# Whole loads of wo and w1, a bf16 turn of the result, and 3/8 of w2's last block in small loads on four DMA engines

## The chip, the cores and the metric

One core of a Trainium2 chip. The metric is the device time of one execution in microseconds (us). A run also has a span, which the profile takes over the program's own instructions; the time is longer than the span by 1.25 to 1.4 us in most runs, and that surplus becomes a subject below. Before: 420.07 us, the median of 3 runs (420.02 to 420.12).

## The reference

A decode step for two sequences of one token: a modulated layernorm, attention of 32 query heads over 4 cached key and value heads of 32768 positions, then an MLP with gelu. Cut to what matters:

```python
mod = (_silu(c) @ w_mod).reshape(c.shape[0], 6, 1, -1)      # sa, ca, ga, sb, cb, gb
h = _layernorm(x) * (1 + ca) + sa
x = x + ga * attention(h, k_cache, v_cache, wq, wo)          # wo: 4096 x 1024
h = _layernorm(x) * (1 + cb) + sb
x = x + gb * (gelu(_layernorm(h) @ w1 + b1) @ w2 + b2)       # w1: 1024 x 3584, w2: 3584 x 1024
```

All is bf16. A "turn" below is a transpose made on TensorE. 178 MB are read, 134 MB of them the caches; the last 22 MB are wo (8), w1 (7) and w2 (7).

## The kernel before

All big operands pass through one ring of 160 KB per partition, in the order wmod, wq, eight rounds of K, K, V, wo, w1, w2. An item is loaded as soon as the readers of what stood in its place are done. What the change touches:

```python
W2_ITEMS = ((0, 8, 96), (8, 16, 112), (16, 24, 128), (24, 27, 144), (27, 28, 150))   # blocks, place in KB
# ...
for m, off in enumerate((128, 0)):
    add(("wo", m), [16, DM], A_wo[m * 2048:(m + 1) * 2048, :].rearrange("(p j) n -> p j n", j=16), off * KB)
w1_v = B_w1.rearrange("(p k) n -> p k n", k=KT8)
for m, off in enumerate((32, 64)):
    add(("w1", m), [4, F], w1_v[:, 4 * m:4 * m + 4, :], off * KB)
w2_v = B_w2.rearrange("(p j) n -> p j n", j=FT)
for m, (j0, j1, off) in enumerate(W2_ITEMS):
    add(("w2", m), [j1 - j0, DM], w2_v[:, j0:j1, :], off * KB)
# ... attention, wo, layernorm, w1, gelu -> gT ...
for g in range(16):                       # blocks 0-15 as rows: gT is the stationary operand
    for hf in range(2):
        # ... pe: matmul(psS[0][32*t : 32*t+32, :], lhsT=gT[:, g, :], rhs=w[:, j, hf*512:(hf+1)*512])
load_row("dve", psS[0], "psS0", 3)        # copy out of PSUM
to_columns(psO, "psO", 3, True, False)    # four f32 matmuls turn the rows into columns
for g in range(16, FT):                   # blocks 16-27 as columns: w2 is the stationary operand
    for k in range(KT8):
        # ... pe: matmul(psO[:, 2*k:2*k+2], lhsT=w[:, j, k*128:(k+1)*128], rhs=gT[:, g, 0:2])
# dve: mT = psO * gb ; res_bf = mT + x1b
pe(lambda e: e.matmul(psM[0:16, 0:128], lhsT=res_bf.rearrange("p b k -> p (b k)"), rhs=ident[:, :], start=True, stop=True),
   reads=["res_bf", "ident"], writes=["psM"])
dve(lambda e: e.tensor_copy(res16[:, :], psM[0:16, 0:128]), reads=["psM"], writes=["res16", "c16"])
```

Below, "item one" to "item five" are the five loads of w2.

## Time and profile before

| | before |
|---|---|
| time, median of 3 | 420.07 us |
| span of the profile | 418.7 us |
| DMA | busy in all 40 slices, 426 GB/s over the span |
| last load of w2 lands | 415.76 us |
| result stored | 418.7 us |

The profile's page and its views are quoted in the prediction, with what each line says. Two things are needed besides. Each load leaves landing marks in the trace, taken here as one for each DMA engine that it uses (16 for item four; the four-row load of b2 has 4 and an early one), in the order of time and without the engine's number; a load counts as landed with the last. And the chain of waits gives, for each piece, start, length and what was done or waited for; "DMA w" is the wait for a load of w1 or w2.

### The profile page before, as it was taken

Reading aid. Unit: us, or ns where it says so; the run is one execution under the profiler, and the core shown is the slowest. Engines: PE = TensorE matmul, PEld = TensorE weight load, DVE = VectorE, ACT = ScalarE, POOL = GpSimd, SP = SyncE. Lnnn points to the kernel's source line nnn. Section 1 sums busy time; section 2 is a strip of 40 time slices with the busy share of each in tenths; the row PEclk is TensorE's granted clock in tenths of the full one; section 3 lists DMA queues with packets and bytes.
Section 4 is the critical chain, followed back from the end, with each engine's and each line's share of the span. In section 5 each row is a group of like instructions: output and inputs, shape, how many; then the busy total and the mean of one; then the engine's idle time right before and its main releaser. Section 6 shows DMA issues by size and latency. Waiting matters only on the chain.

```text
span 418.7 us, 11609 instructions
## 1 busy us (share of the span) xinstructions
PE 291.0 (70%) x5183; PEld 231.3 (55%) x5183; DVE 209.6 (50%) x423; ACT 149.4 (36%) x179; POOL 6.8 (2%) x29
## 2 busy tenths in 40 slices
PE   1407449766996895699369957976995699564536
PEld 1104219762993794299149926962894399221214
DVE  1201105546677676467726664766477567620411
ACT  2000015533565364256405632643365166400100
POOL 3000000000000000000000000000000000000000
PEclk9999557986896997799589958986697889576585
DMA  9989999999999999999999999999999999899995
GB/s 373 450 380 449 448 404 493 398 406 446 441 432 429 423 451 429 419 454 457 391 435 476 407 416 448 438 438 426 438 438 426 416 460 457 377 448 428 424 427 249
DMA packets 5581, 178.42 MB, mean 426 GB/s; under 512 B 698, under 2 KB 706, under 8 KB 964
## 3 DMA queue, kind: packets, MB, share of 16 engines
q1 hardware_dynamic: 5572, 178.28, 98.8%
q8 instruction: 8, 0.13, 0.1%
q14 instruction: 1, 0.01, 0.0%
HBM read 178.28 MB, written 0.00 MB: 426 GB/s over the span
## 4 chain that ended last, share of the span: by engine, by line
DMA 71%; PE 24%; DVE 2%; issue 1%; ACT 1%; SPq 1%
DMA V<-in_A_v_cache_dram 39%; DMA wo<-in_A_wo_dram 10%; DMA K<-in_A_k_cache_dram 10%; PE psZ L584 10%; DMA w<-in_B_w_dram 9%; PE psKT L536 8%; DMA wmod<-in_w_mod_dram 4%; PE psS L548 1%; PE psZ L548 1%; PE psS L655 1%; PE psZ L729 1%; PE psZ L469 1%; ACT KT_sb L540 0%; PE psS L469 0%; DVE m1c L553 0%
## 5 line engine op out<-in xcount | busy, mean ns | idle before, releaser
L536 PE MATMUL psKT<-ident,K 128*128 128x128 bf16 x2048 | 163.1, 229 | 11.5 <-DMA K<-in_A_k_cache_dram 11.5
L540 ACT ACTIVATE KT_sb<-psKT 128x1024 bf16<-128x1024 bf16 x96 | 98.2, 1025 | 124.4 <-PE psKT L536 124.4
L542 DVE COPY KT_sb<-psKT 128x1024 bf16<-128x1024 bf16 x160 | 106.7, 688 | 61.6 <-PE psKT L536 61.2
L536 PEld LDWEIGHTS psKT<-ident,K 128*128 128x128 bf16 x2048 | 126.7, 102 | 13.0 <-DMA K<-in_A_k_cache_dram 12.7
L584 PE MATMUL psZ<-V,E_sb 128*32 128x512 bf16 x512 | 46.4, 541 | 23.2 <-DMA V<-in_A_v_cache_dram 20.0
L548 PE MATMUL psS<-qcur,KT_sb 128*128 128x8 bf16 x1024 | 44.7, 167 | 2.2 <-issue 2.2
L584 PEld LDWEIGHTS psZ<-V,E_sb 128*32 128x32 bf16 x512 | 18.7, 130 | 47.7 <-issue 38.8
L548 PE MATMUL psZ<-qcur,KT_sb 128*128 128x8 bf16 x1024 | 43.0, 167 | 2.2 <-issue 1.5
L548 PEld LDWEIGHTS psS<-qcur,KT_sb 128*128 128x128 bf16 x1024 | 40.0, 97 | 2.3 <-issue 2.3
L548 PEld LDWEIGHTS psZ<-qcur,KT_sb 128*128 128x128 bf16 x1024 | 37.9, 96 | 3.4 <-issue 1.6
L572 ACT ACTIVATE E_sb<-S_sb 128x512 bf16<-128x512 f32 x32 | 19.5, 630 | 29.6 <-DVE S_sb L570 29.6
L570 DVE TENSOR_TENSOR S_sb<-S_sb,gmb 128x512 f32<-128x512 f32 x32 | 20.0, 685 | 0.3
L576 DVE TENSOR_REDUCE rs<-E_sb 128x8 f32<-128x512 bf16 x32 | 19.7, 675 | 0.0
L469 PE MATMUL psS<-wmod,inT 128*32 128x512 bf16 x32 | 5.1, 624 | 16.2 <-DMA wmod<-in_w_mod_dram 16.2
L553 DVE TENSOR_REDUCE m1c<-psZ 128x8 f32<-128x512 f32 x16 | 11.1, 693 | 10.2 <-ACT S_sb L552 10.1
L595 DVE RECIPROCAL rinv<-psM 128x1 f32<-128x1 f32 x8 | 1.3, 168 | 27.7 <-PE psM L593 27.7
L605 PE MATMUL psM<-msum,hmat 128*128 128x128 f32 x16 | 4.2, 347 | 13.3 <-DVE msum L600 13.3
L559 PE MATMUL psM<-identf,m 128*8 128x128 f32 x16 | 4.3, 369 | 13.1 <-DVE m L556 13.1
L553 DVE TENSOR_REDUCE m1c<-psS 128x8 f32<-128x512 f32 x16 | 11.1, 693 | 3.2 <-ACT S_sb L552 3.1
L552 ACT ACTIVATE S_sb<-psZ 128x512 f32<-128x512 f32 x16 | 9.5, 595 | 7.5 <-PE psZ L548 7.5
L477 DVE COPY S_sb<-psS 128x512 f32<-128x512 f32 x1 | 0.7, 690 | 22.9 <-PE psS L469 22.9
L469 PEld LDWEIGHTS psS<-wmod,inT 128*32 128x32 bf16 x32 | 1.1, 132 | 19.3 <-DMA wmod<-in_w_mod_dram 18.0
(123 smaller groups left out, 167.5 us busy)
## 6 DMA issues: line engine op xcount, KB each, us to landing
K<-in_A_k_cache_dram SPq DMA_DIRECT2D x16, 4096.0 KB, 27.1
wq<-in_A_wq_dram SPq DMA_DIRECT2D x2, 4096.0 KB, 44.8
wo<-in_A_wo_dram SPq DMA_DIRECT2D x2, 4096.0 KB, 39.0
w<-in_B_w_dram SPq DMA_DIRECT2D x2, 3584.0 KB, 32.5
wmod<-in_w_mod_dram SPq DMA_DIRECT2D x1, 6144.0 KB, 29.8
w<-in_B_w_dram SPq DMA_DIRECT2D x3, 2048.0 KB, 37.8
wmod<-in_w_mod_dram SPq DMA_DIRECT2D x1, 4608.0 KB, 15.8
wmod<-in_w_mod_dram SPq DMA_DIRECT2D x1, 1536.0 KB, 6.0
```

Source lines behind the costliest of these rows:

```text
L469: pe(lambda e, w=it.view, k=k, kk=kk, ch=ch, n=n, q=q: e.matmul(bank[n][32 * q:32 * q + 32, :], lhsT=inT[:, k, :], rhs=w[:, kk, ch * 512:( ...
L536: pe(lambda e, kq=kq, jj=jj, w=kt, t=t: e.transpose(psKT[kq][:, jj * 128:(jj + 1) * 128], w[:, t, :], ident[:, :]), reads=[it.reg, "ident" ...
L540: act(lambda e, src=src: e.activation(KT_sb[g8][:, :, :], src, ACT.Copy), reads=[f"psKT{kq}"], writes=[f"KT_sb{g8}"], sem=f"ev{cc}_{g8}")
L542: dve(lambda e, src=src: e.tensor_copy(KT_sb[g8][:, :, :], src), reads=[f"psKT{kq}"], writes=[f"KT_sb{g8}"], sem=f"ev{cc}_{g8}")
L548: pe(lambda e, t=t, jj=jj: e.matmul(ps[:, t * HPG:(t + 1) * HPG], lhsT=KT_sb[g8][:, jj, :], rhs=qcur[:, :], start=True, stop=True), reads= ...
L552: act(lambda e: e.activation(Sc, ps.rearrange("p (t h) -> p h t", h=HPG), ACT.Copy), reads=[preg], writes=[f"S_sb_{cc}"], sem=f"sc{cc}")
L553: dve(lambda e: e.tensor_reduce(m1c[:, :, cc], ps.rearrange("p (t h) -> p h t", h=HPG), AX.X, ALU.max), reads=[preg], writes=[f"m1c{cc}"])
L559: pe(lambda e: e.matmul(psM[0:HPG, 0:128], lhsT=m1[:, :], rhs=identf[:, :], start=True, stop=True), reads=["m1", "identf"], writes=["psM"])
L570: dve(lambda e: e.tensor_tensor(Sc, Sc, gmb[:, :].unsqueeze(2).to_broadcast([128, HPG, TPC]), ALU.subtract), reads=[f"S_sb_{cc}", "gmb"], ...
L572: act(lambda e: e.activation(Ec, Sc.rearrange("p h (u t) -> p u h t", t=4), ACT.Exp, scale=SCALE), reads=[f"S_sb_{cc}"], writes=[f"E_sb_{c ...
L576: dve(lambda e: e.tensor_reduce(rs4[:, :, cc], Ec.rearrange("p u h t -> p h u t"), AX.XY, ALU.add), reads=[f"E_sb_{cc}"], writes=[f"rs4_{c ...
L584: pe(lambda e, t4=t4, tg=tg, q=q: e.matmul(psO[32 * q:32 * q + 32, :], lhsT=E_sb[:, tg // 4, :, :].rearrange("p h t -> p (h t)"), rhs=vt[: ...
```

## The change

The intent: half of the 16 DMA engines end 1.3 us before the other half, so part of the last bytes is moved to four engines, by small loads into partitions 0-15 and 32-47; fewer, longer loads for wo and w1; a cheaper last copy. Two row blocks of w2 become column blocks. The core of the diff, with the tables of the attention output (which now hold four groups instead of two) cut:

```diff
-W2_ITEMS = ((0, 8, 96), (8, 16, 112), (16, 24, 128), (24, 27, 144), (27, 28, 150))
+W2_ITEMS = ((0, 8, 64), (8, 16, 80), (16, 24, 0), (24, 27, 16), (27, 28, 22))
+W2_ROWS = 14
+W2_CUT = 640
 ...
-    for m, off in enumerate((128, 0)):
-        add(("wo", m), [16, DM], A_wo[m * 2048:(m + 1) * 2048, :]..., off * KB)
-    for m, off in enumerate((32, 64)):
-        add(("w1", m), [4, F], w1_v[:, 4 * m:4 * m + 4, :], off * KB)
+    add(("wo", 0), [32, DM], A_wo.rearrange("(p j) n -> p j n", j=32), 0)
+    add(("w1", 0), [8, F], B_w1.rearrange("(p k) n -> p k n", k=KT8), 104 * KB)
     for m, (j0, j1, off) in enumerate(W2_ITEMS):
-        add(("w2", m), [j1 - j0, DM], w2_v[:, j0:j1, :], off * KB)
+        n1 = W2_CUT if j1 == FT else DM
+        add(("w2", m), [j1 - j0, n1], w2_v[:, j0:j1, 0:n1], off * KB)
 ...                                          # after the matmuls of wo:
+    for q in range(4):
+        for h in range(2):
+            src = w2_v[32 * q + 16 * h:32 * q + 16 * h + 16, FT - 1, W2_CUT:DM].rearrange("(b a) n -> a b n", a=4)
+            T.dma("sp", ... e.dma_start(w2x[32 * h:32 * h + 16, q, :], src), ...)
 ...                                          # 14 row blocks; before the ninth: gx = the rows of gT that belong to w2x
+            for q in range(4):
+                pe(... e.matmul(psM[0:48, 56 + 2 * q:58 + 2 * q], lhsT=selp[:, q, :], rhs=gT[:, FT - 1, 0:2], ...))
 ...                                          # blocks 14 and 15 as columns, then
+    for q in range(4):
+        for k in range(W2_CUT // 128, KT8):
+            pe(... e.matmul(psO[:, 2 * k:2 * k + 2], lhsT=w2x[:, q, ...], rhs=gx[:, q, :], start=False, stop=False))
 ...
-    pe(... e.matmul(psM[0:16, 0:128], lhsT=res_bf..., rhs=ident[:, :], start=True, stop=True) ...)
-    dve(lambda e: e.tensor_copy(res16[:, :], psM[0:16, 0:128]), ...)
+    pe(... e.transpose(psKT[0][0:16, 0:128], res_bf..., ident[:, :]) ...)
+    dve(lambda e: e.tensor_copy(res16[:, :], psKT[0][0:16, 0:128]), ...)
```

More of the change, by code (lines that the diff above doesn't have):

```diff
@@ L258, in bass_adaLN_cond__gqa_block_cached__mixer_channel_mlp__decode_kernel @@
     onesf = sb("onesf", [128, 128])
-    hmat = sb("hmat", [128, 2, HPG, 8])
+    hmat = sb("hmat", [128, G, HPG, 4])
     hsel = sb("hsel", [128, HPG])
     mk4 = sb("mk4", [128, 4])
-    m8 = sb("m8", [128, 8])
+    m8 = sb("m8", [128, 4])
     mblk = sb("mblk", [128, KT8])
@@ L265, in bass_adaLN_cond__gqa_block_cached__mixer_channel_mlp__decode_kernel @@
     c16 = sb("c16", [16, 128], BF16)
-    rsum16 = sb("rsum16", [128, 2, HPG, 8])
+    rsum16 = sb("rsum16", [128, G, HPG, 4])
     msum = sb("msum", [128, 128])
@@ L289, in bass_adaLN_cond__gqa_block_cached__mixer_channel_mlp__decode_kernel @@
     qcur = sb("qcur", [128, HPG], BF16)
-    at = sb("at", [128, 16], BF16)
-    atT = [sb(f"atT{i}", [128, 16, 32], BF16) for i in range(G // 2)]
+    at = sb("at", [128, 32], BF16)
+    atT = sb("atT", [128, 32, 32], BF16)
     half = sb("half", [128, 2, 2])
@@ L301, in bass_adaLN_cond__gqa_block_cached__mixer_channel_mlp__decode_kernel @@
     res16 = c16
+    w2x = sb("w2x", [48, 4, DM - W2_CUT], BF16)
+    gx = sb("gx", [48, 4, 2], BF16)
+    selp = sb("selp", [128, 4, 48], BF16)
     m1c = sb("m1c", [128, HPG, NCH])
@@ L367, in bass_adaLN_cond__gqa_block_cached__mixer_channel_mlp__decode_kernel @@
         add_v(i)
-    for m, off in enumerate((128, 0)):
-        add(("wo", m), [16, DM], A_wo[m * 2048:(m + 1) * 2048, :].rearrange("(p j) n -> p j n", j=16), off * KB)
-    w1_v = B_w1.rearrange("(p k) n -> p k n", k=KT8)
-    for m, off in enumerate((32, 64)):
-        add(("w1", m), [4, F], w1_v[:, 4 * m:4 * m + 4, :], off * KB)
+    add(("wo", 0), [32, DM], A_wo.rearrange("(p j) n -> p j n", j=32), 0)
+    add(("w1", 0), [8, F], B_w1.rearrange("(p k) n -> p k n", k=KT8), 104 * KB)
     w2_v = B_w2.rearrange("(p j) n -> p j n", j=FT)
     for m, (j0, j1, off) in enumerate(W2_ITEMS):
-        add(("w2", m), [j1 - j0, DM], w2_v[:, j0:j1, :], off * KB)
+        n1 = W2_CUT if j1 == FT else DM
+        add(("w2", m), [j1 - j0, n1], w2_v[:, j0:j1, 0:n1], off * KB)
     w2_of = {j: (m, j - j0) for m, (j0, j1, off) in enumerate(W2_ITEMS) for j in range(j0, j1)}
@@ L411, in bass_adaLN_cond__gqa_block_cached__mixer_channel_mlp__decode_kernel @@
     T.inst("pool", lambda e: e.memset(onesf[:, :], 1.0), writes=["onesf"])
-    for t, nm in [(inT, "inT"), (gT, "gT")] + [(atT[g], f"atT{g}") for g in range(G // 2)]:
+    T.inst("pool", lambda e: e.memset(selp[:, :, :], 0.0), writes=["selp"])
+    for h in range(2):
+        T.inst("pool", lambda e, h=h: e.tensor_copy(selp[:, :, 32 * h:32 * h + 16].rearrange("p q (a b) -> p q a b", a=4),
+                                                    ident.rearrange("p (q h b a) -> p h q a b", q=4, h=2, a=4)[:, h]),
+               reads=["ident"], writes=["selp"])
+    T.inst("pool", lambda e: e.memset(w2x[:, :, :], 0.0), writes=["w2x"])
+    for t, nm in ((inT, "inT"), (gT, "gT"), (atT, "atT")):
         T.inst("pool", lambda e, t=t: e.memset(t[:, :, :], 0.0), writes=[nm])
@@ L451, in bass_adaLN_cond__gqa_block_cached__mixer_channel_mlp__decode_kernel @@
     dve(lambda e: e.tensor_reduce(hsel[:, :], identf.rearrange("p (c h t) -> p h c t", c=4, h=HPG), AX.XY, ALU.add), reads=["identf"], writes=["hsel"])
-    dve(lambda e: e.tensor_copy(hmat[:, :, :, :], hsel[:, :].unsqueeze(1).unsqueeze(3).to_broadcast([128, 2, HPG, 8])), reads=["hsel"], writes=["hmat"])
-    dve(lambda e: e.tensor_reduce(m8[:, :], identf.rearrange("p (h e) -> p e h", e=8), AX.X, ALU.add), reads=["identf"], writes=["m8"])
+    dve(lambda e: e.tensor_copy(hmat[:, :, :, :], hsel[:, :].unsqueeze(1).unsqueeze(3).to_broadcast([128, G, HPG, 4])), reads=["hsel"], writes=["hmat"])
+    dve(lambda e: e.tensor_reduce(m8[:, :], identf.rearrange("p (h e) -> p e h", e=4), AX.X, ALU.add), reads=["identf"], writes=["m8"])
     dve(lambda e: e.tensor_reduce(mblk[:, :], identf.rearrange("p (k u) -> p k u", u=16), AX.X, ALU.add), reads=["identf"], writes=["mblk"])
@@ L527, in next_q @@
         b, g = i % 2, i // 2
-        T.inst("pool", lambda e: e.tensor_copy(qcur[:, :], qT[:, b, g * HPG:(g + 1) * HPG]), reads=["qT"] + [f"atT{g}" for g in range(G // 2)], writes=["qcur"], sem="qc")
+        T.inst("pool", lambda e: e.tensor_copy(qcur[:, :], qT[:, b, g * HPG:(g + 1) * HPG]), reads=["qT", "atT"], writes=["qcur"], sem="qc")
     def tr(i, cc, g8):
@@ L591, in row_sums @@
         dve(lambda e: e.tensor_reduce(rowsum[:, :], rs4[:, :, :], AX.X, ALU.add), reads=[f"rs4_{cc}" for cc in range(NCH)], writes=["rowsum"])
-        dve(lambda e: e.tensor_copy(rsum16[:, :, :, :], rowsum[:, :].unsqueeze(1).unsqueeze(3).to_broadcast([128, 2, HPG, 8])), reads=["rowsum"], writes=["rsum16"], sem="rs")
+        dve(lambda e: e.tensor_copy(rsum16[:, :, :, :], rowsum[:, :].unsqueeze(1).unsqueeze(3).to_broadcast([128, G, HPG, 4])), reads=["rowsum"], writes=["rsum16"], sem="rs")
         pe(lambda e: e.matmul(psM[:, 144:145], lhsT=rsum16.rearrange("p g h e -> p (g h e)"), rhs=onesf[:, 0:1], start=True, stop=True),
@@ L606, in extract_2 @@
            reads=["hmat", "msum"], writes=["psM"])
-        dve(lambda e: e.scalar_tensor_tensor(out=pick[:, :, :], in0=psM[:, 256:384].rearrange("p (e j) -> p e j", j=16), scalar=rinv[:, 0:1],
-                                             in1=m8[:, :].unsqueeze(2).to_broadcast([128, 8, 16]), op0=ALU.mult, op1=ALU.mult),
+        dve(lambda e: e.scalar_tensor_tensor(out=pick.rearrange("p e j -> p (e j)").rearrange("p (e j) -> p e j", j=32), in0=psM[:, 256:384].rearrange("p (e j) -> p e j", j=32), scalar=rinv[:, 0:1],
+                                             in1=m8[:, :].unsqueeze(2).to_broadcast([128, 4, 32]), op0=ALU.mult, op1=ALU.mult),
             reads=["psM", "rinv", "m8"], writes=["pick"], sem="pk")
@@ L612, in red @@
             with nc.allow_low_precision("one nonzero term in each sum"):
-                return e.tensor_reduce(at[:, :], pick.rearrange("p e j -> p j e"), AX.X, ALU.add)
+                return e.tensor_reduce(at[:, :], pick.rearrange("p e j -> p (e j)").rearrange("p (e j) -> p j e", j=32), AX.X, ALU.add)
         dve(red, reads=["pick"], writes=["at"])
-        lo = 64 * (g % 2)
-        T.inst("pool", lambda e: e.tensor_copy(atT[g // 2][lo:lo + 64, :, b], at[lo:lo + 64, :]), reads=["at"], writes=[f"atT{g // 2}"], sem="ac")
+        lo = 32 * g
+        T.inst("pool", lambda e: e.tensor_copy(atT[lo:lo + 32, :, b], at[lo:lo + 32, :]), reads=["at"], writes=["atT"], sem="ac")
     rounds = {}
@@ L648, in bass_adaLN_cond__gqa_block_cached__mixer_channel_mlp__decode_kernel @@
     T.dma("sp", lambda e: e.dma_start(b1m[:, :], B_b1.rearrange("(q r) -> q r", r=448)), key="ld_b1", writes=["b1m"])
-    for m in range(2):
-        it = need("wo", m)
-        for j in range(16):
-            for hf in range(2):
-                q = 2 * (j % 2) + hf
-                pe(lambda e, w=it.view, m=m, j=j, hf=hf, q=q: e.matmul(psS[0][32 * q:32 * q + 32, :], lhsT=atT[m][:, j, :], rhs=w[:, j, hf * 512:(hf + 1) * 512],
-                                                                       start=(m == 0 and j < 2), stop=(m == 1 and j >= 14), skip_group_check=True),
-                   reads=[it.reg, f"atT{m}"], writes=["psS0"], mark=(j == 15 and hf == 1))
+    it = need("wo", 0)
+    for j in range(32):
+        for hf in range(2):
+            q = 2 * (j % 2) + hf
+            pe(lambda e, w=it.view, j=j, hf=hf, q=q: e.matmul(psS[0][32 * q:32 * q + 32, :], lhsT=atT[:, j, :], rhs=w[:, j, hf * 512:(hf + 1) * 512],
+                                                              start=(j < 2), stop=(j >= 30), skip_group_check=True),
+               reads=[it.reg, "atT"], writes=["psS0"], mark=(j == 31 and hf == 1))
+    for q in range(4):
+        for h in range(2):
+            src = w2_v[32 * q + 16 * h:32 * q + 16 * h + 16, FT - 1, W2_CUT:DM].rearrange("(b a) n -> a b n", a=4)
+            T.dma("sp", lambda e, q=q, h=h, src=src: e.dma_start(w2x[32 * h:32 * h + 16, q, :], src), key=f"ld_w2x{q}{h}", reads=["w2x"], writes=[f"w2x{q}{h}"])
     def load_row(e_name, b, b_reg, n, parts=128):
@@ L691, in bass_adaLN_cond__gqa_block_cached__mixer_channel_mlp__decode_kernel @@
     for k in range(KT8):
-        it = need("w1", k // 4)
+        it = need("w1", 0)
         for n in range(2):
@@ L695, in bass_adaLN_cond__gqa_block_cached__mixer_channel_mlp__decode_kernel @@
                 lo = 896 * q + 448 * n
-                pe(lambda e, w=it.view, k=k, n=n, q=q, lo=lo: e.matmul(zbank[n][32 * q:32 * q + 32, 0:448], lhsT=inT[:, k, :], rhs=w[:, k % 4, lo:lo + 448],
+                pe(lambda e, w=it.view, k=k, n=n, q=q, lo=lo: e.matmul(zbank[n][32 * q:32 * q + 32, 0:448], lhsT=inT[:, k, :], rhs=w[:, k, lo:lo + 448],
                                                                        start=False, stop=(k == KT8 - 1), skip_group_check=True),
@@ L713, in bass_adaLN_cond__gqa_block_cached__mixer_channel_mlp__decode_kernel, with w2_columns @@
     dve(lambda e: e.tensor_tensor(x1b[:, :, :], x1b[:, :, :], x1T[:, :, :], ALU.add), reads=["x1b", "x1T"], writes=["x1b"])
-    for g in range(16):
+    def w2_columns(g, start):
+        m, j = w2_of[g]
+        it = need("w2", m)
+        for k in range(KT8 if g < FT - 1 else W2_CUT // 128):
+            pe(lambda e, w=it.view, g=g, j=j, k=k: e.matmul(psO[:, 2 * k:2 * k + 2], lhsT=w[:, j, k * 128:(k + 1) * 128], rhs=gT[:, g, 0:2],
+                                                            start=(start and k == 0), stop=(g == FT - 1 or (g == FT - 2 and k >= W2_CUT // 128)), skip_group_check=True),
+               reads=[it.reg, "gT"], writes=["psO"], mark=((k == KT8 - 1 and g in (15, 23, 26)) or (g == FT - 1 and k == W2_CUT // 128 - 1)))
+    for g in range(W2_ROWS):
+        if g == 8:
+            for q in range(4):
+                pe(lambda e, q=q: e.matmul(psM[0:48, 56 + 2 * q:58 + 2 * q], lhsT=selp[:, q, :], rhs=gT[:, FT - 1, 0:2], start=True, stop=True),
+                   reads=["selp", "gT"], writes=["psM"], mark=(q == 3))
+            act(lambda e: e.activation(gx[:, :, :], psM[0:48, 56:64].rearrange("p (q b) -> p q b", b=2), ACT.Copy), reads=["psM"], writes=["gx"])
         m, j = w2_of[g]
@@ L720, in bass_adaLN_cond__gqa_block_cached__mixer_channel_mlp__decode_kernel @@
             pe(lambda e, w=it.view, g=g, j=j, hf=hf, t=t: e.matmul(psS[0][32 * t:32 * t + 32, :], lhsT=gT[:, g, :], rhs=w[:, j, hf * 512:(hf + 1) * 512],
-                                                                   start=(g < 2), stop=(g >= 14), skip_group_check=True),
-               reads=[it.reg, "gT"], writes=["psS0"], mark=(hf == 1 and g in (7, 15)))
+                                                                   start=(g < 2), stop=(g >= W2_ROWS - 2), skip_group_check=True),
+               reads=[it.reg, "gT"], writes=["psS0"], mark=(hf == 1 and g in (7, W2_ROWS - 1)))
@@ L723, in bass_adaLN_cond__gqa_block_cached__mixer_channel_mlp__decode_kernel @@
     load_row("dve", psS[0], "psS0", 3)
-    to_columns(psO, "psO", 3, True, False)
-    for g in range(16, FT):
-        m, j = w2_of[g]
-        it = need("w2", m)
-        for k in range(KT8):
-            pe(lambda e, w=it.view, g=g, j=j, k=k: e.matmul(psO[:, 2 * k:2 * k + 2], lhsT=w[:, j, k * 128:(k + 1) * 128], rhs=gT[:, g, 0:2],
-                                                            start=False, stop=(g == FT - 1), skip_group_check=True),
-               reads=[it.reg, "gT"], writes=["psO"], mark=(k == KT8 - 1 and g in (23, 26, 27)))
+    for g in range(W2_ROWS, 16):
+        w2_columns(g, g == W2_ROWS)
@@ new lines, in bass_adaLN_cond__gqa_block_cached__mixer_channel_mlp__decode_kernel @@
+    for q in range(4):
+        for k in range(W2_CUT // 128, KT8):
+            pe(lambda e, q=q, k=k: e.matmul(psO[:, 2 * k:2 * k + 2], lhsT=w2x[:, q, k * 128 - W2_CUT:(k + 1) * 128 - W2_CUT], rhs=gx[:, q, :],
+                                            start=False, stop=False, skip_group_check=True),
+               reads=[f"w2x{q}0", f"w2x{q}1", "w2x", "gx"], writes=["psO"], mark=False)
+    to_columns(psO, "psO", 3, False, False)
+    for g in range(16, FT):
+        w2_columns(g, False)
@@ L732, in bass_adaLN_cond__gqa_block_cached__mixer_channel_mlp__decode_kernel @@
     dve(lambda e: e.tensor_tensor(mT[:, :, :], psO[:, 0:16].rearrange("p (k b) -> p k b", b=2), mod(5), ALU.mult), reads=["psO", "modT"], writes=["mT"])
     dve(lambda e: e.tensor_tensor(res_bf.rearrange("p b k -> p k b"), mT[:, :, :], x1b[:, :, :], ALU.add), reads=["mT", "x1b"], writes=["res_bf"])
-    pe(lambda e: e.matmul(psM[0:16, 0:128], lhsT=res_bf.rearrange("p b k -> p (b k)"), rhs=ident[:, :], start=True, stop=True),
-       reads=["res_bf", "ident"], writes=["psM"])
-    dve(lambda e: e.tensor_copy(res16[:, :], psM[0:16, 0:128]), reads=["psM"], writes=["res16", "c16"])
+    pe(lambda e: e.transpose(psKT[0][0:16, 0:128], res_bf.rearrange("p b k -> p (b k)"), ident[:, :]), reads=["res_bf", "ident"], writes=["psKT0"])
@@ L738, in bass_adaLN_cond__gqa_block_cached__mixer_channel_mlp__decode_kernel @@
+    dve(lambda e: e.tensor_copy(res16[:, :], psKT[0][0:16, 0:128]), reads=["psKT0"], writes=["res16", "c16"])
     s_out = nc.alloc_semaphore("s_out")
```

## The prediction

A is 415.47 - 415.12 = +0.35, less 0.08 and 0.06, so +0.2 on 420.07; B is -0.06 - 0.08 - 0.06 = -0.2; 419.9 was forecast. That C's extra matmuls would raise the clock is the author's estimate. In before, each of the 18 rises from half to full clock follows a step of 3.41 us with the PE busy for 80 to 100% of it; the step from 408.98 was busy for 2.62 of 3.42 us, 77%, and half clock followed.

> **What bounds the kernel now.** I read the page first: the slices and the DMA queues.
>
> ```profile
> DMA  9989999999999999999999999999999999899995
> GB/s 373 450 380 449 448 404 493 398 406 446 441 432 429 423 451 429 419 454 457 391 435 476 407 416 448 438 438 426 438 438 426 416 460 457 377 448 428 424 427 249
> ...
> q1 hardware_dynamic: 5572, 178.28, 98.8%
> q8 instruction: 8, 0.13, 0.1%
> ...
> HBM read 178.28 MB, written 0.00 MB: 426 GB/s over the span
> ```
>
> The 16 DMA engines are busy from the first slice to the last but one, so the span is the bytes at about 430 GB/s, plus what lies before the first byte and after the last. The change removes no bytes. It can only win or lose in the last microseconds, so next the chain of waits over the last 6 us (start, length, what):
>
> ```profile
> 375.40 37.83 DMA w<-in_B_w_dram
> 413.23 0.05 issue
> 413.27 1.87 PE psZ L729 x64
> 415.14 0.03 issue
> 415.17 1.03 PE psZ L729 x32
> 416.20 0.02 issue
> 416.22 0.19 DVE mT L732
> ...
> 416.43 0.24 DVE res_bf L733
> ...
> 416.72 0.29 PE psM L734
> ...
> 417.03 0.28 DVE c L736
> ```
>
> w2's third item (blocks 16 to 23) lands at 413.23 and 64 matmuls on columns follow, then the rest. Then a closing chain of four short operations, about 1.1 us, and the store (median 1.4 us to landing). The view of the tile w (count, min/median/max ns, first and last start) and the timeline near the end say how that work runs:
>
> ```profile
> L729 PE MATMUL psZ<-gT,w x96: 165/165/188, 413.3 to 416.0; 128*128 128x2 bf16 x96
> ...
> L720 PE MATMUL psS<-w,gT x32: 377/498/634, 403.7 to 409.7; 128*32 128x512 bf16 x32
> ...
> DMA to landing us min/median/max: 29.8/37.8/39.5
> ```
>
> From the single starts in the trace, a column matmul starts every 0.0267 us and takes 0.165 us (the granted clock is half from 405.57 on). The 64 of blocks 16 to 23 start from 413.27 to 414.98; the next starts only at 415.17, because the fourth item (24 to 26) lands at 415.12. After that nothing waits: the last item lands at 415.76, before its 25th matmul since 415.17. So the end hangs on the landing of item four, plus 32 matmuls: 415.12 + 0.05 + 31 x 0.0267 + 0.165 = 416.17, against 416.20 in the chain.
>
> **Who lands late.** Each load leaves 16 landing marks in the trace, one for each DMA engine. For item four they are: seven at 413.47 to 413.86, one at 414.38, eight at 414.86 to 415.12. For the last item: seven at 414.11 to 414.49, one at 415.01, eight at 415.47 to 415.76. Half of the engines are done 1.3 us before the others: that slack is what the change wants. It comes from the instruction queue: its eight packets of 16 KB (36.4, 63.2, 75.1, 82.6, 89.5, 98.1, 386.1, 407.1 us) each make one more engine late. wq's second half had one late engine, the K load landing at 101.4 had six; w1's first half, after 386.1, had seven; item three, after 407.1, has eight. The middle one is only 0.5 us behind the fast ones; it appears at the V load landing at 91.7 us, after the 8 KB packet on another queue at 84.8 us.
>
> [...]the four b2 loads (1, 2, 4 and 1 rows) have 1, 2, 4 and 1 marks from data plus an early one, and b1 (8 rows) 8 plus one. The new small loads have a source of 4 x 4 x 384[...]. [...] No view shows an engine's number. [...]the clock records here change in steps of 3.41 us between 1.0 and 0.5.
>
> [...]The b2 load of four rows landed at 360.96, 361.18, 361.47 and 361.75, just behind the last V load (fast engines 360.63 to 361.12, the middle one 361.56, late ones from 362.07). Successive small loads on one engine land 0.18 to 0.19 apart: 360.82, 361.00, 361.18, 361.37, 361.57[...]. So three of the four are fast, but one (361.75 - 0.19 = 361.56) is the middle one. This is inference from marks, and it is the point on which the sign hangs.
>
> **The change part by part.**
> - *wo and w1 in one load each.* Fixed cost of a load from landings: the fifth item (256 KB) took 415.76 - 415.12 = 0.64, the fourth (768 KB) 1.89; slope 1.25 per 512 KB, so 0.64 - 0.625 = 0.015 fixed; two K loads, 2 x 9.69, against one V load of the same bytes, 19.35, give 0.03. I take 0.03: two loads fewer, -0.06 us on every engine. Its price: wo's 64 matmuls now wait for all of wo (381.7). At half clock 16 in 1.71 us (0.427 per four), at full 0.215 per four; with the clock up at 385.09 they end at about 387.1, against 385.28. The layernorm chain moves from 385.3-395.7 to 387.1-397.5; w1, landed whole at 398.7, still comes after it. Then all 64 w1 matmuls (0.373 per four cold, 0.19 warm) run to about 404, against 400.6, and gelu takes 2.2 more: gT at 406.2, against 402.7. w2's second item lands only at 408.4, so this hides, with about 2 us left.
> - *Issue.* wo now waits for the last K's use (355.0) instead of the first half going at 331; V keeps the engines to 360.6. w1 waits for V's use (368.9) while wo flows to 380. Item three waits for wo's use (387) while w1 flows to 397. No gap.
> - *14 row blocks, 16 column matmuls, 4 + 12 new ones.* Four 512-column matmuls less; 28 x 0.0267 = 0.75 us of column work lies beside the 0.69 us row copy; the eight f32 turns (1.87) end near 412.6, before 413.2. Hidden.
> - *3/8 of the last block.* The other twelve engines move 10 KB for it instead of 16: 0.625 x 3/8 = -0.23 us on item five. But item five is not the one waited for; there the gain is the three matmuls fewer, 3 x 0.0267 = -0.08.
> - *The eight small loads.* 24.6 KB more on each of four engines at 27.1 GB/s (4 MB in 9.67 us over 16) is 0.91, plus 8 x 0.03 = 1.15 us, issued behind wo and so in front of all of w1 and w2. On the three fast engines item four lands at 413.9 + 1.15 at most, 415.0: free. On the middle one 414.38 + 1.15 - 0.06 = 415.47, which is 0.35 later than the 415.12 that sets the end now.
> - *bf16 turn.* The f32 copy of 16x128 out of PSUM is 0.28 us; the main loop's bf16 copy of 1024 elements takes 0.69, about 0.5 ns an element where f32 takes 1 (0.69 for 512). 128 elements cheaper by half: -0.06. The turn itself stays at 0.29.
>
> **Rivals.** (A) The middle engine is one of the four: item four at 415.47, end +0.35 - 0.08 - 0.06 = +0.2, so 420.3; with the small loads at pure bandwidth (0.91) it is about -0.03. (B) The four are all fast, or the 8 KB packet falls on another engine this time: the late engines set the end, -0.06 - 0.08 - 0.06 = -0.2, so 419.87. (C) The extra matmuls from 408 to 412 bring the clock up at 412.4: 28 remaining starts at some 0.022 (a score matmul's 8 in 0.18 in the loop) save 0.13 more, and it helps A as well as B; against it, the same window of before was busy two thirds and stayed at half. (D) The delayed wo and w1 work sets the end: needs 2 us more than worked out; then +0.5 to +2. For A speak the marks; for B only that 3/8 (0.91 us by bytes) fits the 1.3 us of slack of the fast engines.
>
> **Range and chances.** A and B about even, a little C: 419.9 us, a shade below 420.07. Eight in ten: 419.4 to 420.5; repeats of before agree within 0.1. Two per cent is 8.4 us and the whole tail after the last DMA byte is under 4 us, so only a gap in the loads could leave that band. Faster 0.01, within 0.98, slower 0.01.
>
> **What would show it.** Right: DMA slices as before up to the last, item five's late marks 0.2 to 0.3 earlier, four marks of every load behind wo later by about 1.1 us, w1's matmuls in one run from about 399 to 404, the PE idle before w2's third item, the copy at 0.2. A is shown by one mark of item four near 415.5 with the PE waiting for it; B by eight marks at 415.06 as the last. Wrong: a DMA gap near 355-380; column turns ending after 413.2; another instruction packet after 408 on one of the four engines; or small loads that cost 0.2 us each, not 0.14, and hold all their engines back.

## The result

The changed kernel took 420.41 us, the median of 6 runs (420.09 to 421.06); before, in 6 runs, 420.14 (420.02 to 420.28). The ratio is 1.0009, 95% interval 0.9996 to 1.0021: the same within 2%, and if anything slower. A ratio here is the mean time of one kernel's fast runs over that of the other's of the same rounds, so not quite the ratio of the medians. Differences of 0.1% lie within such an interval; what carries the argument is the pattern of the landing marks and the spans. Single marks move too: item four's last one lies anywhere from 414.94 to 415.21 in the five profiles with whole loads of wo and w1 and no small ones, so a shift of 0.1 in one profile means little.

The page of the changed kernel, slices and queues:

```profile
DMA  9989999999999999999999999999999999999995
...
q1 hardware_dynamic: 5444, 178.28, 98.7%
q8 instruction: 9, 0.15, 0.1%
```

The loads are as dense as before and move the same bytes: no gap has opened by the later issue of wo and w1. One instruction packet more than before (9, not 8). Now the chain of waits over the last microseconds of the changed kernel. The start of the first "issue" piece is the landing that ended the wait:

```profile
388.09 25.63 DMA w<-in_B_w_dram
413.72 0.05 issue
413.76 2.79 PE psZ L732 x93
416.55 0.02 issue
416.57 0.18 DVE mT L760
...
416.78 0.24 DVE res_bf L761
...
417.06 0.29 PE psKT L762
...
417.38 0.21 DVE c L763
```

Item three lands at 413.72 instead of 413.23, and mT starts at 416.57 instead of 416.22, 0.35 later, though there are 93 matmuls instead of 96. The last copy takes 0.21 instead of 0.28. The sum, the end of that copy, is 417.59 against 417.31: +0.28, and that is the difference of the spans (419.0 against 418.7).

The marks of item four, the load that decides, one for each engine (read from the traces, us):

```
before   413.47 413.50 413.54 413.59 413.64 413.77 413.86 | 414.38 | 414.86 414.87 414.88 414.89 414.96 415.00 415.07 415.12
changed  413.46 413.57 413.68 413.76 | 414.63 414.66 414.71 414.79 414.81 414.87 414.90 414.93 415.00 415.05 415.16 | 415.56
```

Three marks have left the fast group for the late one, the one at 414.38 is gone, and a single engine now ends 0.4 us after everybody else. The small loads' own marks say which: the first of them lands at 380.35, 380.52, 380.60 and 381.34, so the fourth engine trails the third by 0.74 from the outset. In the prediction's words this is the middle engine.

The chain shows the 93 matmuls as one piece, but the single starts in the trace have a gap in it, from 415.46 to 415.60: the wait for item four. In thirteen of the fourteen profiles mT starts a nearly fixed time after item four's last mark: 1.09 to 1.13 us where 32 matmuls are left then, 1.04 and 1.05 where 30 are, 1.01 and 1.02 where 29 are. The exception is pad26, below.

The work that the late wo moves, in the timeline of the changed kernel's PE from 409 to 414 (start, length, line, what, count, idle time before and what ended it):

```profile
409.07 1.47 PE L746 MATMUL psS<-w,gT 128*32 128x512 bf16 x12
410.48 0.58 PE L732 MATMUL psZ<-gT,w 128*128 128x2 bf16 x16
411.00 0.48 PE L754 MATMUL psZ<-gx,w2x 48*128 48x2 bf16 x12
411.40 1.87 PE L681 MATMUL psZ<-half,S_sb 128*128 128x4 f32 x8
413.76 0.40 PE L732 MATMUL psZ<-gT,w 128*128 128x2 bf16 x9 [0.49 <-DMA w<-in_B_w_dram]
```

The turns end at 413.27 (411.40 + 1.87) and the PE then idles 0.49 us for item three: still hidden, but with half a microsecond to spare in this profile.

### The profile page after: what moved, and what is told of

Same layout as the page of the kernel before. It is cut to its first block, busy times and chain, and to the rows that moved or that the text cites. A ratio compares the mean times of both kernels' runs of the same rounds, so it can differ in the third digit from the quotient of the medians.

```text
span 419.0 us, 11673 instructions
## 1 busy us (share of the span) xinstructions
PE 290.0 (69%) x5208; PEld 232.7 (56%) x5208; DVE 209.7 (50%) x423; ACT 149.4 (36%) x180; POOL 9.3 (2%) x32
## 4 chain that ended last, share of the span: by engine, by line
DMA 66%; PE 31%; DVE 1%; issue 1%; ACT 1%; SPq 0%
DMA K<-in_A_k_cache_dram 50%; PE psKT L545 21%; DMA wo<-in_A_wo_dram 6%; DMA w<-in_B_w_dram 6%; DMA wmod<-in_w_mod_dram 4%; PE psS L557 4%; PE psZ L557 2%; PE psS L663 2%; PE psZ L593 1%; PE psZ L732 1%; PE psZ L478 1%; PE psS L478 0%; DVE msum L609 0%; ACT KT_sb L549 0%; DVE m1c L562 0%
## 5 line engine op out<-in xcount | busy, mean ns | idle before, releaser
L549 ACT ACTIVATE KT_sb<-psKT 128x1024 bf16<-128x1024 bf16 x96 | 98.1, 1025 | 127.8 <-PE psKT L545 127.8
L593 PE MATMUL psZ<-V,E_sb 128*32 128x512 bf16 x512 | 44.5, 524 | 25.2 <-DMA V<-in_A_v_cache_dram 23.5
L663 PE MATMUL psS<-wo,atT 128*32 128x512 bf16 x64 | 6.3, 577 | 11.1 <-DMA wo<-in_A_wo_dram 11.1
## 6 DMA issues: line engine op xcount, KB each, us to landing
w<-in_B_w_dram SPq DMA_DIRECT2D x1, 768.0 KB, 27.1
```

What stands on the lines that cost most here:

```text
L549: act(lambda e, src=src: e.activation(KT_sb[g8][:, :, :], src, ACT.Copy), reads=[f"psKT{kq}"], writes=[f"KT_sb{g8}"], sem=f"ev{cc}_{g8}")
L593: pe(lambda e, t4=t4, tg=tg, q=q: e.matmul(psO[32 * q:32 * q + 32, :], lhsT=E_sb[:, tg // 4, :, :].rearrange("p h t -> p (h t)"), rhs=vt[: ...
L663: pe(lambda e, w=it.view, j=j, hf=hf, q=q: e.matmul(psS[0][32 * q:32 * q + 32, :], lhsT=atT[:, j, :], rhs=w[:, j, hf * 512:(hf + 1) * 512] ...
```

## The experiments

Theory 1: the small loads take 1.1 to 1.2 us of each of four engines; on three of them that fills slack, on the middle one it makes the last mark of items three to five, and that costs more than the rest of the change gains. Rival 2: the later layernorm and w1 work, which follows from one load of wo, costs the time. Theory 3: the late engines differ from run to run. Theory 5 came up on the way (no theory 4 was put on record): a longer PE program asks for one more instruction block (a 16 KB packet of the instruction queue) near the end, which costs time outside the span. All diffs below are cut. Each kernel gave the right result and had 5 rounds (eng6_640 has 6 runs).

| kernel | time, median (range) | before in the same rounds | ratio, 95% interval | median span | time less span |
|---|---|---|---|---|---|
| merge_only | 419.95 (419.87-420.14) | 420.13 | 0.9996, 0.9983-1.0010 | 418.6 | 1.27-1.35 |
| no_small | 420.55 (420.06-420.65) | 420.13 | 1.0005, 0.9992-1.0019 | 418.6 | 1.46-2.05 |
| small_only | 420.28 (420.27-420.57) | 420.13 | 1.0005, 0.9991-1.0018 | 418.9 | 1.36-1.38 |
| double | 421.58 (421.50-423.01) | 420.13 | 1.0033, 1.0020-1.0047 | 420.2 | 1.38-1.43 |
| merge_turn | 419.86 (419.80-419.95) | 420.12 | 0.9995, 0.9982-1.0008 | 418.6 | 1.26-1.35 |
| eng3_768 | 419.98 (419.84-420.59) | 420.12 | 1.0000, 0.9987-1.0013 | 418.6 | 1.34-1.42, one 1.99 |
| eng6_640 | 421.71 (420.51-422.32) | 420.12 | 1.0030, 1.0017-1.0043 | 419.2 | 1.37-2.89 |
| after_again | 420.33 (420.21-420.55) | 420.12 | 1.0005, 0.9992-1.0018 | 418.9 | 1.37-1.65 |
| pad12 | 419.92 (419.88-420.62) | 420.11 | 0.9998, 0.9984-1.0012 | 418.6 | 1.28-1.92 |
| pad26 | 420.45 (420.15-420.56) | 420.11 | 1.0006, 0.9992-1.0020 | 419.1 | 1.25-1.39 |
| turn_only | 420.09 (420.02-420.12) | 420.11 | 0.9999, 0.9985-1.0012 | 418.8 | 1.29-1.36 |
| eng4_768 | 420.00 (419.93-420.20) | 420.11 | 0.9998, 0.9985-1.0012 | 418.6 | 1.36-1.43 |

Before itself, in each of its three sets of rounds (9, 11 and 9 runs): median span 418.8, time less span 1.26 to 1.38.

### The change without the small loads

```diff
-W2_CUT = 640
+W2_CUT = 1024          # the last block whole; w2x, gx, selp and their instructions removed
```

> The changed kernel without the eight small loads (w2's last block whole, for all engines); wo and w1 in one load, 14 row blocks and the bf16 turn stay. Theory 1 (the small loads make the middle engine of the four the last to land item four): item four lands by 415.1 instead of 415.56, time 0.5 us below the changed kernel, 0.1 to 0.25 below before (two loads less 0.06, turn 0.06). Rival 2 (the late layernorm and w1 work that follows the one load of wo costs the time): within 0.1 of the changed kernel, so 0.2 to 0.3 over before. Theory 3 (which engines are late differs from run to run, and only the small loads make the time feel it): the runs spread over 0.3 us at most, as before's do, where the changed kernel's spread over 1 us.

The chain of waits from the landing of item three:

```profile
413.37 0.05 issue
413.42 2.87 PE psZ L718 x96
```

Item four lands at 415.21, one group of seven, one at 414.39, one of eight, as in before. The median span is 418.6, 0.2 under before's in these rounds and 0.3 to 0.4 under the changed kernel's. So within the span theory 1 holds and rival 2 falls. But the time is 420.55, not 419.9, and by the time alone this run does not separate the two: this kernel alone has 1.46 to 2.05 us between span and time in every run. In its trace an 8 KB packet of the other instruction queue lies at 420.4 us, after the program's end; before has none there. This was the start of theory 5.

### The two whole loads alone

```diff
-    for m, off in enumerate((128, 0)): add(("wo", m), ...)
-    for m, off in enumerate((32, 64)): add(("w1", m), ...)
+    add(("wo", 0), [32, DM], ...)
+    add(("w1", 0), [8, F], ...)
```

> Before with wo and w1 in one load each, nothing else. Theory 1: 0.03 to 0.1 us below before (two loads less of 0.03 each), w1's matmuls in one run from 398.7 to about 405, w2's row blocks up to 410.5, column turns done before item three lands. Rival 2: 0.2 to 0.5 over before.

The chain of waits, in this kernel from the landing of item four:

```profile
415.04 0.04 issue
415.08 1.03 PE psZ L728 x32
...
416.13 0.19 DVE mT L731
```

Item four lands at 415.04 instead of 415.12, and mT starts at 416.13 instead of 416.22. The time is 0.18 us under before's median of the same rounds, a little more than the 0.03 to 0.1 expected, with overlapping ranges. Rival 2, which asked for 0.2 to 0.5 over, is refuted a second time.

### The small loads alone

The w2 part of the change on the kernel before; wo, w1 and the turn stay as they were:

```diff
+W2_ROWS = 14
+W2_CUT = 640
+            T.dma("sp", ... e.dma_start(w2x[32 * h:32 * h + 16, q, :], src), ...)     # and gx, selp, the column matmuls
```

> Before with the small loads and 5/8 of the last block, wo and w1 in two loads each as before, f32 turn. Theory 1: item four lands at 415.5 to 415.6 on one engine, 0.4 later than before's; three matmuls fewer give back 0.08: 0.3 to 0.4 us over before, 420.5. Rival 2: at or below before, -0.1 to -0.2. Theory 3: a spread of 0.5 us or more between runs.

The chain of waits from the landing of item three:

```profile
413.73 0.05 issue
413.77 2.79 PE psZ L736 x93
```

Item four's last mark is at 415.57, alone, 0.38 after the next (415.19): the changed kernel's signature without its other parts. The time is 0.15 over before's median, less than the 0.3 to 0.4 expected; the profiled run (span 419.1) was one of the slower ones, the median span is only 0.1 over before. No spread of 0.5 us either, so nothing for theory 3.

### Twice the small loads

```diff
+            T.dma("sp", ... e.dma_start(w2y[32 * h:32 * h + 16, q, :], src[:, :, 0:DM - W2_CUT - 16]), ...)   # not used
```

> The changed kernel with each small load made twice (the second copy, of 368 columns, is not used). Theory 1: the middle engine lands item four 1.1 to 1.2 us later still, at 416.7, and the three fast ones pass the late ones; time 1.1 to 1.2 us over the changed kernel, 421.5. Rival 2: no change beyond 0.1. If a small load costs pure bandwidth, 0.9.

The chain of waits from the landing of item three:

```profile
414.85 0.05 issue
414.90 2.75 PE psZ L734 x93
```

Item three lands 1.13 later than in the changed kernel (414.85 against 413.72) and item four 1.10 later (416.66 against 415.56), for 23.5 KB more on each engine. The time is 421.58, 1.2 over the changed kernel, as expected. This is clear of noise. Three marks of item four now stand together at 415.94 to 416.02, about where the fast three should be; marks carry no number, so this is inferred. One side effect: w1 was issued only at 378.94 instead of 368.2, and the first marks of w1 stand at 398.05 instead of 397.03, so the unloaded fast engines seem to have run dry for about 1 us; the four loaded ones had their small loads left, it is inferred, which land until 382.72 in the changed kernel even without the second copies. One run took 423.01: there an instruction block at 419.6 us seems to have fallen on an engine of the result's store, whose marks are 419.92 to 420.08 and one at 421.60.

### The best of the parts

```diff
+    pe(... e.transpose(psKT[0][0:16, 0:128], res_bf..., ident[:, :]) ...)                 # on merge_only
+    dve(lambda e: e.tensor_copy(res16[:, :], psKT[0][0:16, 0:128]), ...)
```

> Before with wo and w1 in one load each and the bf16 turn; no small loads, 16 row blocks, so the PE's program is no longer than before's. Theory 1: 0.1 to 0.2 us below before and below merge_only by 0.06 (the last copy 0.21 instead of 0.28), 419.85; eight instruction blocks, nothing after the end. If the bf16 turn brings nothing, as merge_only, 419.95.

The end of its chain of waits:

```profile
413.27 0.05 issue
413.31 2.73 PE psZ L728 x96
...
416.07 0.19 DVE mT L731
...
416.87 0.21 DVE c L734
```

419.86 us against 420.12 for before in the same rounds, that is -0.26; its five runs (419.80 to 419.95) all lie under the eleven of before (420.00 to 420.36), though the interval of the ratio, 0.9982 to 1.0008, still holds 1. It has eight instruction blocks, as before. It beats both kernels by median, and it is the version that I would keep.

### Three engines instead of four

```diff
-W2_CUT = 640
+W2_CUT = 768
-            src = w2_v[... 16 rows ...].rearrange("(b a) n -> a b n", a=4)     # eight loads, partitions 0-15, 32-47
+        src = w2_v[r0:r0 + 4 * na, FT - 1, W2_CUT:DM].rearrange("(b a) n -> a b n", a=na)   # na = 3 (last: 2), eleven loads, 0-11, 32-43
```

> The changed kernel with 2/8 of the last block's columns in eleven small loads on three engines (groups of 12 rows, partitions 0-11 and 32-43), so that the middle engine gets none. Theory 1 with the middle engine as number 3: no engine but the eight late ones sets item four, it lands at 415.05 to 415.2, and the engine at 414.35 stays where it was; span 418.6 to 418.8, 0.3 to 0.4 below the changed kernel's profile. If the middle engine is another of the four, one mark of item four stands at 415.5 again and nothing is won.

The chain of waits from the landing of item three:

```profile
413.31 0.05 issue
413.35 2.78 PE psZ L735 x94
```

The small loads have three marks each after the early one, all together (380.39, 380.44, 380.51), and item four has four marks at 413.36 to 413.65, one at 414.42 where the middle engine always stood, and eleven from 414.73 to 415.11. So the middle engine is the fourth (the expectation's number 3, counted from 0), and without a load of its own it harms nobody: the span is the 418.6 of no_small. The win ends there, because the eight late engines set the end in any case.

This is also the clearest answer to rival 2. The kernel keeps the late wo and w1 work, the 14 row blocks and a ninth instruction block (at 416.16), and each of its three engines carries about as much as each of the four did: 21.8 KB, 0.81 us by bytes, and eleven loads of 0.03, some 1.1 us (an estimate by the prediction's figures). Only the middle engine is spared, and the median is 419.98, against 420.33 for the changed kernel in the same rounds (one of the five runs took 420.59, 1.99 longer than its span).

### Six engines

```diff
-W2_CUT = 768            # eng3_768
-NE = 3
+W2_CUT = 640
+NE = 6                  # six loads of 24 rows, the last of 8
```

> The changed kernel with the same bytes in six small loads on six engines (groups of 24 rows, partitions 0-23 and 32-55). Each of the six carries 16 KB and six loads, 0.6 + 6 x 0.03 to 0.04 = 0.8 us instead of 1.15: theory 1 puts the middle engine's item four at 415.15 to 415.2, span 418.65 to 418.8. If a small load's fixed cost rather than its bytes were what holds the engine, 6 of 8 loads leave 0.9, 415.25. Rival 2: as the changed kernel.

The chain of waits from the landing of item three:

```profile
413.85 0.05 issue
413.90 2.79 PE psZ L735 x93
```

A miss: item four at 415.69, not 415.2, and span 419.2. The marks give the reason. The first small load lands at 380.21, 380.45, 380.50, 380.57, 381.08 and 381.90: one of the two added engines is a late one, 0.8 behind the middle. I had taken both for early ones without a reading that said so: the same fault as in the prediction, on a smaller scale. The lesser dose on the middle engine could not be told from this run. The times, 420.51 to 422.32, have the worst tail: an instruction block at 421.0 in the profiled run (time less span 2.89), and two runs with spans of 420.7 and 420.9.

### The changed kernel again

No edit.

> The changed kernel once more, to see whether the middle engine is the same in another profile. Theory 1: the fourth mark of each small load again trails the other three by 0.7 to 0.8, item four's last mark at 415.5 to 415.6, 420.4. Theory 3 (which engines are late changes from run to run): another order of the marks, and an item four anywhere from 415.0 to 416.3.

The chain of waits from the landing of item three:

```profile
413.63 0.05 issue
413.68 2.80 PE psZ L732 x93
```

The fourth mark of each small load trails again (380.29, 380.53, 380.59, 381.26), item four ends at 415.49 with the next at 415.10, and the time is 420.33. In all fourteen profiles the four-row b2 load has its last mark 0.24 to 0.66 us behind the third. So one of the four is the middle one every time, and eng3_768 says that it is the fourth; theory 3, by which the engines change places, falls for it. How far the middle engine trails does vary: its mark in wo's last load, before any small load, lies at 380.87 to 381.13. What remains of a spread is in the last instruction block: at 419.6 in this run, with 1.65 us between span and time, and 1.37 to 1.43 in the other four.

### A longer PE program

```diff
+        if g == 8:
+            for _ in range(12):      # pad26: 26
+                pe(... e.matmul(psM[0:48, 56:58], lhsT=ident[:, 0:48], rhs=gT[:, FT - 1, 0:2], ...), mark=False)   # not used
```

> merge_turn with 12 idle column matmuls (24 PE instructions, the number by which no_small's PE program is longer) put beside the wait for w2's second item; their result is not used. Theory 5 (the time beyond the span is an instruction block or refill that a longer PE program asks for around the end): span as merge_turn's, 418.5 to 418.6, but time less span 1.45 to 2.05 as in no_small, so 420.0 to 420.6. If it was the row and column split that cost no_small its gain: time as merge_turn, 419.8 to 419.95.

Two of five runs have 1.92 and 1.68 us between span and time, the profiled one of them with an 8 KB packet at 420.3, as in no_small; the other three are at 1.28 to 1.32, as merge_turn. So 24 instructions more on the PE are enough for what no_small suffers, but not in every run, as it does there. Half a confirmation.

> merge_turn with 26 idle column matmuls (52 instructions; the changed kernel has 50 more than before). Theory 5: a ninth 16 KB instruction block around 416 to 420, span 418.5 to 418.7, time less span 1.35 to 1.45 in most runs, with one or two at 1.6 to 2.9 or a span 1.5 longer (store behind the block), as in the changed kernel, eng3_768 and eng6_640. Against it: all runs as merge_turn, 1.26 to 1.35.

Confounded by my own edit. The ninth block comes, at 416.6, and leaves the surplus at 1.25 to 1.39, but the span is 419.1, because 26 matmuls at that place use up the PE's half microsecond (0.45 in merge_turn, whose turns end at 412.82). The chain of waits:

```profile
412.87 1.28 PE psZ L667 x6
414.15 2.57 PE psZ L732 x96
```

The turns run to 414.15 while item three had landed at 413.36. No DMA stands in the end of this chain any more: this is what rival 2 would look like if it were true, and it tells how near the changed kernel is to it.

Over all profiles the pattern is this: where an instruction packet lies after the program's end (no_small, pad12, after_again, eng6_640) the surplus of that run is 1.65 to 2.89; where there is none, or it comes before the store (from 416.1 to 416.6), it is 1.30 to 1.43. In double's profiled run the packet fell into the store and lengthened the span instead. Which of these a longer program gets varies from run to run. What exactly the end of the execution waits for is not shown by these traces and stays open.

### The bf16 turn alone

```diff
-    pe(... e.matmul(psM[0:16, 0:128], lhsT=res_bf..., rhs=ident[:, :], start=True, stop=True) ...)      # on before
+    pe(... e.transpose(psKT[0][0:16, 0:128], res_bf..., ident[:, :]) ...)
```

> Before with the bf16 turn alone: the last copy 0.21 instead of 0.28, so 0.05 to 0.1 us below before, 420.03; nothing else moves.

420.09 against 420.11: nothing to be seen in the time of these rounds, though the copy is 0.21 us as expected. From merge_only to merge_turn, in other rounds, the median fell by 0.09. 0.07 is at the edge of what these runs resolve.

### A smaller dose

```diff
-W2_CUT = 640
+W2_CUT = 768
```

> The changed kernel with 2/8 instead of 3/8 of the columns in the eight small loads. Theory 1, by dose: each of the four engines carries 16.4 KB, 0.60, plus 8 x 0.03 to 0.04: 0.85 to 0.9 instead of 1.15; the middle engine lands item four at 415.2 to 415.3, span 418.7, between no_small and the changed kernel. If the dose does not matter: 415.5.

The chain of waits from the landing of item three:

```profile
413.23 0.05 issue
413.28 2.81 PE psZ L732 x94
```

Item four's last mark is at 415.07, 0.1 to 0.2 earlier than expected, and no engine stands apart; median span 418.6. A third fewer bytes, and the loss is gone. Item four's last mark by dose, none 414.94 to 415.21, 2/8 415.07, 3/8 415.56 and 415.49, and twice that 416.66, is what a threshold would give: until the middle engine (at 414.39 without a load) reaches the late ones at 415.1, some 0.7 us, its load is hidden; above it the load counts in full. Why 2/8 cost no more than that 0.7, where 0.85 was expected, can be read from wo: in this profile the middle engine stood at 380.88 before its small loads, against 381.13 and 381.04 in the two profiles of the changed kernel. In no_small it went from 381.04 on wo to 414.39 on item four without a load; by the same step it would have landed here at 414.23, and 0.85 more gives 415.08 (an estimate), among the late ones. So where exactly the threshold lies is not tested by this profile.

## Why the prediction was right or wrong

The sign was wrong: 419.9 was forecast, a shade below before, and 420.41 came, 0.27 above before in the same rounds; the stated range of 419.4 to 420.5 held the median, but not the two slowest of its six runs. Point by point:

- *The step that failed is the path taken for the end of the loads: that the eight late engines land item four last, at 415.06 (rival B).* In the runs these engines are done by 415.16, and one other engine, the middle one with its small loads, lands item four at 415.56 (415.49 in after_again, 415.57 in small_only): rival A. The prediction had worked this out from the marks, called it "the point on which the sign hangs" and derived 420.3, and then set it aside because the packet might fall elsewhere and because 3/8 seemed to fit the slack. All fourteen profiles show a lone middle mark before any small load, and eng3_768 shows whose it is.
- *The forecast does not follow from its own weights.* "A and B about even" gives the mean of 420.3 and 419.87, which is 420.1 and no gain. 419.9 is B's number; from 420.1 even the whole of C (0.13) does not reach it, and only A's cheaper variant, the small loads at 0.91, would. So evenness was stated, but nearly B was forecast.
- *A's own figure, 420.3, was within about 0.1 of the result.* The mechanism was right; A has +0.28 over before, the two profiled runs differ by 0.36, and the rest is the surplus past the span, which A left out.
- *Cost of the small loads*: 1.15 us an engine was expected. In w1's marks the middle engine goes from 397.95 without them (no_small) to 399.15 with them (399.07 in after_again): 1.20 and 1.12. But it already stood at 381.13 and 381.04 on wo, against 381.04 in no_small; corrected for that, 1.11 and 1.12, so 0.91 for bytes and about 0.025 for each load. Item four: 415.47 expected, 415.56 and 415.49 measured. Right. The marks of the small loads themselves come 0.2 apart on one engine (eight from 381.34 to 382.72, and as far apart in eng4_768 with a third fewer bytes), so their distance is not what they cost.
- *Three matmuls fewer, -0.08*: 0.0267 each holds (item four to mT is 1.10 before, 1.01 after). Right.
- *Whole loads, -0.06*: item four moved by -0.08 in merge_only, which is within what the marks vary by; its time moved by -0.18 and its median span from 418.8 to 418.6, with overlapping ranges. Right in sign; the size is not resolved.
- *bf16 turn, -0.06*: the copy went from 0.28 to 0.21. Right on the trace, not resolved in time.
- *Hidden layernorm and w1 work, with "about 2 us left"*: hidden, but mis-sized. wo's matmuls ended at 388.03 (387.1 expected), gT was ready at 407.2 (406.2), the turns ended at 413.27 (412.6). The clock rose at 387.14, not 385.09, so more matmuls ran at half speed (0.427 us for four of wo's before the rise, 0.22 after it). So 1.6 us were left between gT and w2's second item (408.83) instead of 2, and 0.49 between the turns and item three, where the prediction's own figures left 0.6 (1.56 in after_again, whose clock was at full from 410.01 to 413.42). pad26 used up what merge_turn had of it.
- *Rival C, a warm clock at the end*: did not happen in the profiled run; the half clock holds from 407.62, though the PE was busy in all of the step from there to 411.03 and for 2.92 us of the 3.41 after it. So the estimate of what raises the clock is not borne out by this trace. In after_again, no_small and merge_only the clock did rise, at 410.0 to 410.8, but it fell back at 413.4 to 414.2, before item four landed, and mT still started 1.02 to 1.10 after that landing.
- *Not priced in the prediction*: the ninth instruction block. Another packet after 408 stands among the signs of being wrong, but without a cost. It goes with about 0.08 more surplus in kernels that fetch it before the store (1.35 to 1.40 in five of the six first runs of the changed kernel, median 1.30 to 1.32 before) and with 0.3 to 0.6 more in some runs (1.96 and 1.65 in one run of each set). It is not why the changed kernel's first six runs spread over 1 us and before's over 0.3: the spans alone go from 418.7 to 419.5. That spread stays open; a middle engine that trails by more or less from run to run is a candidate, but those runs have no trace.

Together: +0.35 at mT, -0.07 for the copy, about +0.08 past the span make the +0.36 by which the two profiled runs differ (420.38 against 420.02).

## What to carry to other kernels

In this kernel, whose DMA is busy in all 40 slices, the last mark of a load decided and not the mean: mT started 1.01 to 1.13 us after item four's last mark in thirteen of fourteen profiles, and the changed kernel's single mark at 415.56, 0.40 behind the next, cost it the gain. Before giving extra bytes to "the early engines", read from marks of small loads which engines these are, and leave out any that is not early. If a step of an argument rests on such a reading, weigh it by how directly it was read, not by how well the alternative fits the intent. A few more instructions at the end of the program went with a longer time here where one more instruction packet lay after the program's end (1.65 to 2.89 us between span and time in four profiled runs, against 1.30 to 1.43 elsewhere).

## What the traces show of the DMA engines

- After each of the 16384-byte packets of the instruction queue (0.88 to 0.96 us each in before) one more mark of the large loads stands about 1.3 to 1.5 us behind the fast ones, and the late marks stay: in before 1 in wq's second half (after 36.4 us; 52.75 against 51.15 to 51.60), 6 in the K load that lands at 101.36 (after 98.1 us), 8 in item three (after 407.1 us). That the packet makes an engine late is inferred from this order in time.
- A load that stands in a queue behind others took here, besides its bytes, about 0.025 to 0.033 us of each engine that it uses, an estimate: 1.11 us for eight small loads, of which 0.91 is bytes; 1.13 (item three in double against the changed kernel) for the second eight, of which 0.87 is bytes. Bytes are taken at 27.1 GB/s an engine, from 4 MB in 9.67 us over 16.
- Small loads with 4, 3 and 6 rows in the slowest dimension of their source left 4, 3 and 6 marks from data (changed kernel, eng3_768, eng6_640), and each one early mark (357.63 for the first of the changed kernel).
- The middle mark is first seen after an 8 KB packet of the other instruction queue, q14 (at 84.80 us in before, 82.54 in the changed kernel): in before the K load that lands at 72.31 has none, the V load at 91.70 has it at 90.98, and in the loads after it stands 0.4 to 0.8 us behind the last fast mark (371.33 against 370.87 in wo's first half; 100.74 against 99.93 in the changed kernel). That it is this packet is inferred from the time at which the mark appears.
